# Fused HGRN2 attention and SERF feed-forward: an early weight piece, another rounding rate, masks on VectorE, clamps apart from the logs, and the last store in two parts

## The chip, the cores and the metric

The kernel runs on one core of a Trainium2 chip. The time is device time in microseconds of one launch; a run is one execution, and the median of the runs counts. The profile is of one execution of its own.

## The reference

```python
def _attn_ref(q, k, v, f_logit):            # each (4, 8, 768, 48)
    f = 1.0 / (1.0 + np.exp(-f_logit))
    state = np.zeros((B, H, D, D))
    for t in range(S):
        state = f[:, :, t, :, None] * state + einsum('bhd,bhe->bhde', k[:, :, t], v[:, :, t])
        y[:, :, t] = einsum('bhd,bhde->bhe', q[:, :, t], state)

def _moe_ref(x, w_in, w_out):               # (3072, 384), (384, 2048), (2048, 384)
    h = x @ w_in
    sp = np.maximum(h, 0.0) + np.log1p(np.exp(-np.abs(h)))
    return (h * erf(sp)) @ w_out            # x is y with the heads side by side
```

The inputs q, k, v and f_logit are float32. The two weights are float64; the kernel reads them as pairs of 32-bit words and rounds them to float32 itself.

## The kernel before

The sequence is cut into 24 chunks of 128 tokens, six per batch entry. Two chunks form a block of 256 tokens, so there are 12 blocks. A chunk g passes four stages, each a function:

- `stage_d(g)` multiplies the logs of the decays (`lt`) with a triangle on TensorE (L380), takes two exponentials on ScalarE (`dp` L383, `kd` L386), sends the decays of both half chunks to `Tall` by eight small DMAs (L391, from chunk 3 on), and scales q and k on VectorE (`qd` L395, `kd` L399).
- `stage_t(g)` transposes both on TensorE (L411) and copies them out of PSUM: `qA` on ScalarE (L418), `kT` on ScalarE (L420) up to chunk 8 and on VectorE (L422) after.
- `stage_s(g)` computes the state's increments (L460) and the scores (L468). The scores are masked by a triangle: on VectorE in four instructions (L496), or, for chunks 3 to 9, copied by ScalarE in four instructions (L488) and masked by GpSimd in two (L491). Then the state of the half chunk is updated on VectorE (L438, L439, two of each); the state of the other half is left to the next `stage_t`.
- `stage_y(g)` multiplies scores and state with q (L525) and ScalarE copies the result into `xT` (L529).

Ahead of `stage_d`, `prepare` turns logits into logs of the decays: VectorE clamps them (L360), then ScalarE takes Exp (L364) and Ln (L365). For the first two blocks this is done per chunk.

The feed-forward part of a block is `hidden(blk, gi)` for four groups gi: twelve products of `xT` with `w_in_sb` (L587), each two records in the profile, a copy out of PSUM (L594), and the activation in steps: Exp (L157), two Tanh (L160), two VectorE products (L165), a Tanh (L559) and the last product (L561). The projection with w_out is `project_first` (L670) for blocks 0 and 1 and `project` (L718) after, which needs seven products in place of eight and sums of weights (`sum_w`, L615) and of activations.

A weight is loaded in pieces (`load_piece`, L292, eight of w_in with 768 KB each, then eight of w_out) and rounded by `round_piece`: a copy on ScalarE (L311) and six VectorE instructions (L313, L317, L322, L326, L331, L336). `weights_step` issues one of these seven at a time. Piece p of w_in serves the products of two of the sixteen column tiles, so group 0 of a block needs pieces 0 and 1, group 1 needs 2 and 3, and so on.

Nothing is scheduled at run time: every engine and every DMA queue executes its instructions in the order in which the program issues them, and SP's queue issues almost all DMAs. After an opening written out by hand, with loads, the stages of chunks 0 to 2 and ten rounding steps, a loop over rounds `it` walks a generator of products ("slots": one product of L587, L670 or L718 each). Round 0 has 96 slots in the order of groups h0[0], h0[1], h1[0], h0[2], h1[1], h0[3], h1[2], h1[3] of blocks 0 and 1, round 1 the 48 of block 2, round 2 the 48 of block 3 and then the 32 of the first projection. After given slots (`at`) the loop issues the next stage from `todo`; `prepare` for a later block goes 14 slots ahead of that block's first `stage_d`; and a counter `due` grows by a rate per slot and issues one rounding step whenever it reaches one.

Two products of the stages and of the hidden groups take turns in two PSUM buffers each (`ps_at` for d, t and y; `ps_moe` for hidden groups and projections). The last projection adds its seven partial products (`plus`, L726) and writes 256 rows by one DMA (`store`, L654).

Of the kernel before, what the change touches and what calls it, by code (L numbers as in the profile page):

```python
# [43 lines left out]
FP32 = mybir.dt.float32  # L44
# [26 lines left out]
P = 128  # L71
# [3 lines left out]
def kernel(  # L75
# [10 lines left out]
    nc = tc.nc  # L86
# [142 lines left out]
    def load(g, what="qkv", queue=None):  # L229
        b, c = divmod(g, NCH)  # L230
        queue = queue or nc.sync
        for src, t, n in ((q, qns[g % NQ], "q"), (k, kns[g % NQ], "k")):
            if n in what:
                queue.dma_start(out=t[:].rearrange("t (h d) -> t h d", d=D), in_=heads(src, b, c))
        if "v" in what:
            queue.dma_start(
                out=vts[g % NV][:].rearrange("t (h d) -> t h d", d=D), in_=heads(v, b, c)
            )
# [104 lines left out]
    def use_exp_ln():  # L343
        if sets[0] == EXP_LN:
            return
        sets[0] = EXP_LN
        nc.scalar.add_instruction(
            mybir.InstLoadActFuncSet(
                act_func_set_id=EXP_LN, name=nc.get_next_instruction_name(),
                engine=mybir.EngineType.Activation, ins=[], outs=[],  # L350
            )
        )
# [1 line left out]
    def other_set():  # L354
        sets[0] = 0

    def prepare(blk, j0, j1):

        lt = lts[blk][:, j0:j1, :].rearrange("t j c -> t (j c)")
        nc.vector.tensor_scalar(  # L360
            out=lt, in0=lt, scalar1=LOGIT_MIN, scalar2=None, op0=ALU.max
        )
        use_exp_ln()
        nc.scalar.activation(out=lt, in_=lt, func=AF.Exp, scale=-1.0)  # L364
        nc.scalar.activation(out=lt, in_=lt, func=AF.Ln, bias=1.0)  # L365

    busy = []

# [74 lines left out]
    def stage_s(g):  # L443
        b, n = divmod(g, NCH)
        last = n == NCH - 1
        if n == 0:
            for r in range(2):
                nc.gpsimd.memset(svs[g % NSV][rows(r), r, 0, :, PAD : PAD + D], 0.0)
        qA, kT = qAs[g], kTs.pop(g)
        ps = ps_sc.tile([P, 2, 512], FP32, name="sc", tag="sc")  # L450

        sc = ps[:, :, 0 : HP * C].rearrange("s r (a t) -> s r a t", t=C)
        dS = ps[:, :, HP * C : HP * (C + D)]
        totals = ps[:, 0, HP * (C + D) : HP * (C + D) + 2 * HP]
        vt, kd = vts[g % NV], kds[g % 2]
        for a in range(HP):
            for c in range(1 if last else 2):
                for r in range(2):
                    h = 2 * a + r
                    nc.tensor.matmul(  # L460
                        dS[rows(r), c, D * a : D * (a + 1)],
                        lhsT=kd[half(c), h, 0:D], rhs=vt[half(c), D * h : D * (h + 1)],
                        start=True, stop=True,
                    )
        for a in range(HP):
            for r in range(2):
                for c in range(2):
                    nc.tensor.matmul(  # L468
                        sc[half(c), r, a, :], lhsT=kT[rows(r), a, half(c)],
                        rhs=qA[rows(r), r, a, half(c)], start=True, stop=True,  # L470
                    )
        if g < FIRST:

            pairs = dps[g % 2][:].rearrange("t (a r) d -> t a (r d)", r=2)
            for a in range(HP):
                nc.tensor.matmul(
                    totals[:, 2 * a : 2 * a + 2], lhsT=pairs[:, a, :], rhs=ident[:, C - 1 : P : C],
                    start=True, stop=True,
                )
            nc.vector.tensor_copy(  # L480
                out=Tall[:, g].rearrange("p c a -> p a c"),
                in_=totals.rearrange("p (a c) -> p a c", c=2),
            )
        for c in range(2):
            for r in range(2):
                if FIRST <= g < 2 * ADJACENT:

                    nc.scalar.copy(out=qA[half(1 - r), r, :, half(c)], in_=sc[half(c), r])  # L488
                    if c == 1:
                        flat = qA[half(1 - r), r].rearrange("s a (c t) -> s (a c) t", c=2)  # L490
                        nc.gpsimd.affine_select(  # L491
                            out=flat, in_=flat, pattern=[[0, 2 * HP], [1, C]], compare_op=ALU.is_ge,
                            fill=0.0, base=0, channel_multiplier=-1,
                        )
                    continue
                nc.vector.tensor_tensor(  # L496
                    out=qA[half(1 - r), r, :, half(c)], in0=sc[half(c), r],
                    in1=tri1[half(c)].unsqueeze(1).broadcast_to((C, HP, C)), op=ALU.mult,
                )
        next_state(2 * g, dS)  # L500
        if not last:
            late[g] = lambda: next_state(2 * g + 1, dS)
# [149 lines left out]
    def store(blk):  # L652
# [3 lines left out]
            in_=rows_sb[:, 0:4, :].rearrange("p (t two) c -> p t (two c)", t=CPB),  # L656
        )

    def project_first(blk):

        ops = ps_moe.tile([P, 2, 512], FP32, name="ops", tag="moe")
        for gi in range(n_g):
            gr = groups[blk, gi]
            for tt in range(CPB):
                for j in range(FG):
                    ft = gi * FG + j
                    assert n_pieces + ft * n_pieces // n_ft in rounded
                    while not gr["done"]:
                        act_step()
                    nc.tensor.matmul(  # L670
                        ops[:, tt, 0:d_model],
                        lhsT=gr["h"][:, j, tt * P : (tt + 1) * P],
                        rhs=w_out_sb[:, ft, :],
                        start=(ft == 0), stop=(ft == n_ft - 1),
                    )
                    if j == FG - 1 and tt == CPB - 1:
                        if blk == 0:
                            to_sum.append(sum_w(gi))
                        if gi == n_g - 1:
                            nc.scalar.copy(  # L680
                                out=rows_sb[:, 0:4, :].rearrange("p (t two) c -> p t (two c)", t=CPB),
                                in_=ops[:, :, 0:d_model],
                            )
                            store(blk)
                    yield

    def project(blk):
# [6 lines left out]
            1: (0, 0, 0), 2: (0, 1, 0), 6: (0, 1, 1), 5: (1, 0, 0), 7: (1, 0, 1), 3: (2, 1, 0), 4: (2, 1, 1),  # L694
        }.items()}
        first = [1, 2, 5, 3]

        def pair(n):
            i, j = {2: (0, 1), 5: (1, 0), 3: (2, 1)}[n]
# [37 lines left out]
        def fives():  # L737

            plus(o[:, 3:5, :], o[:, 4:5, :].broadcast_to((P, 2, DH)), pair(5))

        yield from products((2, 3), (5, 7))
        if end:

            fives()
        yield from products((2, 3), (3, 4))
        if not end:
            fives()
        plus(o[:, 1:3, :], o[:, 3:5, :], pair(3))
        plus(o[:, 3, :], o[:, 3, :], place[7])
        store(blk)  # L750
# [42 lines left out]
    with tc.manual_schedule():  # L793
# [5 lines left out]
        load(0, "kv", nc.scalar)  # L799
        load(0, "q")  # L800
        load_f(1)
        load(1, "qk")
        load_f(2)
        load_piece(0)
        load(1, "v")
        load(2)
        load_piece(1)
        load_piece(2)
        load_f(3)
        nc.gpsimd.memset(tri[:], 1.0)  # L810
# [45 lines left out]
        def weights_steps(n):  # L856
            for _ in range(n):
                weights_step()
# [5 lines left out]
        keep_busy(6)  # L864
        prepare(0, 1, 2)
        stage_t(0)
        load(3, "qk")
        load_piece(3)
        stage_d(1)
# [43 lines left out]
        for it in range(n_blocks):  # L913
            gen, n = slots(it)
            if it == 0:
                todo = [(stage_s, 2), (stage_y, 2), (stage_d, 3), (stage_t, 3), (stage_s, 3), (stage_y, 3),
                        (stage_d, 4), (stage_t, 4), (stage_d, 5), (stage_s, 4), (stage_t, 5),
                        (stage_y, 4)] + stages(2)[4:]
                at = [1, 5, 6, 12, 16, 23, 34, 42, 48, 52, 60, 74, 76, 80, 88, 94]
            else:  # L920
                todo = stages(it + 2) if it + 2 < n_blocks else []
                at = [n * x // 48 for x in (2, 6, 11, 17, 25, 29, 34, 41)] if it == 1 else [int(3 + (n - 13) / max(1, len(todo)) * i) for i in range(len(todo))]
# [5 lines left out]
                prepare_at = at[todo.index((stage_d, (it + 3) * CPB))] - 14  # L928
            at, todo = deque(at), deque(todo)
            for s, _ in enumerate(gen):  # L930
                due += (1 if s < 42 else 0.6 if s < 72 else 0.3) if it == 0 else 0.42 if it == 1 else 0.6
                while due >= 1:
                    weights_step()
                    due -= 1
# [2 lines left out]
                if at and s == at[0]:  # L937
# [3 lines left out]
                    if f in (stage_y, stage_y_s):  # L941
# [3 lines left out]
                        if g == 2:  # L945
                            load(5, "v")
                            load_piece(7)
                if it == 0 and s == 14:
                    prepare(2, 0, CPB)
                if it == 0 and s == 9:  # L950
                    load_f(6)
                    load_f(7)
                if s == n // 2 and it + 4 < n_blocks:
                    for j in range(CPB):
                        load_f((it + 4) * CPB + j)
                if it + 3 < n_blocks and s == prepare_at:
                    prepare(it + 3, 0, CPB)
                if it < 2:
                    step = it == 1 and s % 6 == 3
                elif it == 2:  # L960
# [240 lines left out]
```

## Time and profile before

| | us |
|---|---|
| median of 5 runs (lowest, highest) | 619.28 (618.65, 619.62) |
| the profiled execution | 619.4 |
| its span, first to last instruction | 617.6 |
| TensorE busy / VectorE / ScalarE / GpSimd | 586.9 / 460.5 / 382.4 / 14.4 |
| mean granted TensorE clock | 0.985 |
| L587 products, 1152 records | 265.2 |
| six VectorE rounding instructions of a piece, start to start | 4.64 |

A timeline row reads: start, duration, engine, line, operation, output and inputs, shapes, count, and in brackets the idle time before it with what ended it. A window row reads: stretch and length, busy time of the engines with instruction counts, granted clock, share of the DMA engines, GB/s. Durations of overlapping instructions can reach into each other, so repeated instructions are best counted start to start.

### The profile page before, as it was taken

The numbers are of one execution on the slowest core, as the hardware profiler recorded it, in microseconds if no ns is written. First come the engines' busy times: TensorE is split into PE (matmuls) and PEld (weight loads), VectorE is DVE, ScalarE is ACT, GpSimd is POOL, SyncE is SP. The second block draws the span as 40 slices with busy tenths as digits, with TensorE's granted clock in tenths as the row PEclk, the third lists the DMA queues.
The fourth block names the chain that finished last, engine by engine and source line by source line (L and its number), as shares of the span: only waits on it lengthen the run. The fifth ranks groups of instructions, "written<-read, shape, count | busy, mean of one in ns | idle before, by whom it ended". The sixth has DMA issues, their size and how long they took to land.

```text
span 617.6 us, 13765 instructions
## 1 busy us (share of the span) xinstructions
PE 586.9 (95%) x5729; PEld 513.3 (83%) x5729; DVE 460.5 (75%) x784; ACT 382.4 (62%) x483; POOL 14.4 (2%) x33
## 2 busy tenths in 40 slices
PE   8778799999999999999999999999999999999995
PEld 7656688888655689989989989988988989989995
DVE  5998998697489597896796876896886785647551
ACT  5735357987875778775866685875765566366000
POOL 1000001010000000000000000000000000000000
PEclk9978799999999999999999999999999999999999
DMA  9998753351241223223233132142120000000000
GB/s 198 249 234 215 205 157 62 62 102 16 50 78 27 49 56 52 44 61 54 39 65 53 34 71 53 19 86 53 18 62 14 3 27 0 28 1 0 27 27 29
DMA packets 155587, 41.35 MB, mean 67 GB/s; under 512 B 147328, under 2 KB 150400, under 8 KB 155520
## 3 DMA queue, kind: packets, MB, share of 16 engines
q1 hardware_dynamic: 153440, 40.02, 29.7%
q8 instruction: 47, 0.77, 0.5%
q10 hardware_dynamic: 2080, 0.39, 0.3%
q14 instruction: 20, 0.16, 0.1%
HBM read 35.59 MB, written 4.72 MB: 65 GB/s over the span
## 4 chain that ended last, share of the span: by engine, by line
PE 74%; DVE 14%; ACT 7%; issue 3%; DMA 1%; POOL 0%; ACTq 0%; DVEq 0%; SPq 0%; POOLq 0%
PE hps L587 31%; PE ops L718 25%; PE ops L670 7%; PE y L525 3%; PE ps_t L411 3%; PE ps_d L380 2%; ACT x L160 1%; PE sc L468 1%; PE sc L460 1%; DVE sv L438 1%; DVE sv L439 1%; DVE Hg L561 1%; DVE w_in_sb L322 1%; DVE w_in_sb L336 1%; DVE qA L496 1%
## 5 line engine op out<-in xcount | busy, mean ns | idle before, releaser
L587 PE MATMUL hps<-xT,w_in_sb 128*128 128x256 f32 x1152 | 265.2, 386 | 4.2 <-DVE w_in_sb L336 1.9
L587 PEld LDWEIGHTS hps<-xT,w_in_sb 128*128 128x128 f32 x1152 | 219.1, 193 | 38.6 <-ACT xT L529 2.7
L165 DVE SCALAR_TENSOR_TENSOR e<-x,e 128x1024 f32<-128x1024 f32 x96 | 117.0, 1219 | 13.1 <-ACT x L160 12.6
L160 ACT ACTIVATE x<-Hg,serf_bias 128x1024 f32<-128x1024 f32 x88 | 97.5, 1140 | 0.2
L157 ACT ACTIVATE e<-Hg 128x1024 f32<-128x1024 f32 x44 | 46.5, 1058 | 61.7 <-DVE Hg L561 57.6
L718 PE MATMUL ops<-wT,Hg 128*128 128x192 f32 x320 | 78.9, 328 | 0.0
L561 DVE TENSOR_TENSOR Hg<-Hg,e 128x1024 f32<-128x1024 f32 x44 | 53.8, 1222 | 22.2 <-ACT e L559 22.1
L718 PE MATMUL ops<-wT,scratch 128*128 128x192 f32 x288 | 67.8, 326 | 0.9 <-DVE scratch L726 0.9
L718 PE MATMUL ops<-w_out_sb,Hg 128*128 128x192 f32 x320 | 65.1, 326 | 0.0
L594 ACT COPY Hg<-hps 128x1024 f32<-128x1024 f32 x44 | 44.4, 1009 | 32.8 <-PE hps L587 32.4
L718 PEld LDWEIGHTS ops<-wT,Hg 128*128 128x128 f32 x320 | 55.8, 190 | 1.9
L718 PEld LDWEIGHTS ops<-w_out_sb,Hg 128*128 128x128 f32 x320 | 54.6, 190 | 2.0
L559 ACT ACTIVATE e<-e 128x1024 f32<-128x1024 f32 x48 | 50.3, 1049 | 1.9 <-DVE e L165 1.8
L718 PEld LDWEIGHTS ops<-wT,scratch 128*128 128x128 f32 x288 | 50.3, 190 | 1.1 <-issue 1.1
L496 DVE TENSOR_TENSOR qA<-sc,tri 64x256 f32<-64x256 f32 x68 | 28.7, 422 | 24.5 <-PE sc L468 23.6
L726 DVE TENSOR_TENSOR scratch<-scratch,ops 128x384 f32<-128x384 f32 (+1 forms) x40 | 20.1, 503 | 31.8 <-ACT scratch L734 24.5
L525 PEld LDWEIGHTS y<-qA,sv 128*32 128x32 f32 x1536 | 24.2, 111 | 20.7 <-issue 12.9
L525 PE MATMUL y<-qA,sv 128*32 128x64 f32 x1536 | 29.0, 223 | 12.1 <-issue 4.5
L418 ACT COPY qA<-ps_t 64x512 f32<-64x512 f32 x48 | 27.7, 577 | 19.6 <-PE ps_t L411 19.2
L395 DVE TENSOR_TENSOR qd<-qn,dp 128x384 f32<-128x384 f32 x24 | 13.3, 556 | 32.7 <-ACT dp L383 28.6
L718 PE MATMUL ops<-w_out_sb,scratch 128*128 128x192 f32 x144 | 35.2, 326 | 0.0
L438 DVE TENSOR_TENSOR sv<-sc,sv 48x192 f32<-48x192 f32 x80 | 28.4, 355 | 8.7 <-ACT qA L488 7.3
(111 smaller groups left out, 645.6 us busy)
## 6 DMA issues: line engine op xcount, KB each, us to landing
lt<-in_f_logit_dram SPq DMA_DIRECT2D x24, 192.0 KB, 3.7
qn<-in_q_dram SPq DMA_DIRECT2D x24, 192.0 KB, 3.3
out_dram<-scratch SPq DMA_DIRECT2D x12, 384.0 KB, 2.6
kn<-in_k_dram SPq DMA_DIRECT2D x23, 192.0 KB, 3.5
vt<-in_v_dram SPq DMA_DIRECT2D x23, 192.0 KB, 3.6
sv<-in_v_dram SPq DMA_DIRECT2D x84, 48.0 KB, 2.9
w_out_sb<-in_moe_w_in_dram SPq DMA_DIRECT2D x4, 768.0 KB, 6.3
Hg<-in_moe_w_in_dram SPq DMA_DIRECT2D x4, 768.0 KB, 6.9
```

The lines of the kernel that those rows point to most:

```text
L157: nc.scalar.activation(out=dst[:], in_=h, func=AF.Exp)
L160: nc.scalar.activation(out=dst[:], in_=h, func=AF.Tanh, bias=serf_bias[:, i : i + 1], scale=SERF_KAB[i][0])
L165: nc.vector.scalar_tensor_tensor(out=e[:], in0=x[:], scalar=SERF_KAB[i][2], in1=e[:], op0=ALU.add, op1=ALU.mult)
L438: nc.vector.tensor_tensor(out=new, in0=add, in1=old, op=ALU.add)
L496: nc.vector.tensor_tensor(out=qA[half(1 - r), r, :, half(c)], in0=sc[half(c), r], in1=tri1[half(c)].unsqueeze(1).broadcast_to((C, HP, C)), ...
L525: nc.tensor.matmul(y[M * i : M * (i + 1), kt, half(c)], lhsT=sv[:, r, c, a, o : o + M], rhs=qA[:, r, a, half(c)], start=(n == 0), stop=Tru ...
L559: nc.scalar.activation(out=e[:], in_=e[:], func=AF.Tanh, scale=SERF_C)
L561: nc.vector.tensor_tensor(out=h, in0=h, in1=e[:], op=ALU.mult)
L587: nc.tensor.matmul(hps[:, j, :], lhsT=w_in_sb[:, kt, ft * P : (ft + 1) * P], rhs=xTs[blk][:, kt, :], start=(kt == 0), stop=(kt == n_k - 1),)
L594: nc.scalar.copy(out=gr["h"], in_=hps[:])
L670: nc.tensor.matmul(ops[:, tt, 0:d_model], lhsT=gr["h"][:, j, tt * P : (tt + 1) * P], rhs=w_out_sb[:, ft, :], start=(ft == 0), stop=(ft == ...
L718: nc.tensor.matmul(place[n], lhsT=x[:, j, :], rhs=y, start=(gi == 0 and j == 0 and n in first), stop=(gi == n_g - 1 and j == 1), skip_grou ...
```

## The change

- `prepare` is split into `clamp` (VectorE) and `logs` (ScalarE). In the loop the clamp goes six slots ahead of the logs. For block 2 they go after slots 18 and 24, where both went after 14.
- Masks: only chunks 3 to 5 still go over ScalarE and GpSimd; chunks 6 to 9 use the four VectorE instructions.
- Opening loads: the first w_in piece goes ahead of chunk 1's q, k and v, and the second ahead of chunk 2's logits, q, k and v.
- Two rounding steps are added after `stage_t(0)`; the rate of round 0 is 1 up to slot 18, 0.46 up to 66 and 0.3 after, where it was 1 up to 42, 0.6 up to 72 and 0.3 after; the rate of round 1 is 0.55 (was 0.42) and of later ones 0.55 (was 0.6).
- Round 0 takes `stage_d(3)` ahead of `stage_y(2)`, and moves four of its sixteen stages by one to three slots.
- The last projection keeps product 4 in a PSUM tile of its own, finishes the sum of the first 128 rows before the last four products, and stores 128 rows from SP and 128 from ScalarE.

```diff
-    def prepare(blk, j0, j1):
-
+    def clamp(blk, j0, j1):
         lt = lts[blk][:, j0:j1, :].rearrange("t j c -> t (j c)")
         nc.vector.tensor_scalar(
             out=lt, in0=lt, scalar1=LOGIT_MIN, scalar2=None, op0=ALU.max
         )
+
+    def logs(blk, j0, j1):
+
+        lt = lts[blk][:, j0:j1, :].rearrange("t j c -> t (j c)")
         use_exp_ln()
         nc.scalar.activation(out=lt, in_=lt, func=AF.Exp, scale=-1.0)
         nc.scalar.activation(out=lt, in_=lt, func=AF.Ln, bias=1.0)
+
+    def prepare(*which):
+        clamp(*which)
+        logs(*which)
...
-                if FIRST <= g < 2 * ADJACENT:
+                if FIRST <= g < 2 * FIRST:
...
+    def store_tile(blk, t, queue):
+        r = blk * TB + t * P
+        queue.dma_start(
+            out=out[r : r + P, :],
+            in_=rows_sb[:, 2 * t : 2 * t + 2, :].rearrange("p two c -> p (two c)"),
+        )
...
+        if end:
+            place[4] = ps_at.tile([P, 512], FP32, name="ops4", tag="at")[:, 0:DH]
+            first.append(4)
...
         if end:
 
             fives()
+            yield from products((2, 3), (3,))
+            plus(o[:, 1, :], o[:, 3, :], place[3])
+            store_tile(blk, 0, nc.sync)
+            plus(o[:, 3, :], o[:, 3, :], place[7])
+            yield from products((2, 3), (4,))
+            plus(o[:, 2, :], o[:, 4, :], place[4])
+            store_tile(blk, 1, nc.scalar)
+            return
         yield from products((2, 3), (3, 4))
-        if not end:
-            fives()
+        fives()
...
         load_f(1)
-        load(1, "qk")
+        load_piece(0)
+        load(1, "qkv")
+        load_piece(1)
         load_f(2)
-        load_piece(0)
-        load(1, "v")
         load(2)
-        load_piece(1)
         load_piece(2)
...
         stage_t(0)
+        weights_steps(2)
         load(3, "qk")
...
-                todo = [(stage_s, 2), (stage_y, 2), (stage_d, 3), (stage_t, 3), (stage_s, 3), (stage_y, 3),
+                todo = [(stage_s, 2), (stage_d, 3), (stage_y, 2), (stage_t, 3), (stage_s, 3), (stage_y, 3),
...
-                at = [1, 5, 6, 12, 16, 23, 34, 42, 48, 52, 60, 74, 76, 80, 88, 94]
+                at = [1, 5, 8, 12, 16, 23, 36, 43, 48, 52, 60, 74, 76, 80, 88, 94]
...
-                due += (1 if s < 42 else 0.6 if s < 72 else 0.3) if it == 0 else 0.42 if it == 1 else 0.6
+                due += (1 if s < 18 else 0.46 if s < 66 else 0.3) if it == 0 else 0.55
...
-                if it == 0 and s == 14:
-                    prepare(2, 0, CPB)
+                if it == 0 and s == 18:
+                    clamp(2, 0, CPB)
+                if it == 0 and s == 24:
+                    logs(2, 0, CPB)
...
+                if it + 3 < n_blocks and s == prepare_at - 6:
+                    clamp(it + 3, 0, CPB)
                 if it + 3 < n_blocks and s == prepare_at:
-                    prepare(it + 3, 0, CPB)
+                    logs(it + 3, 0, CPB)
```

## The prediction

> **What bounds the kernel now.** I read the page's busy rows first, then its slices, then the chain of waits.
>
> ```profile
> PE 586.9 (95%) x5729; PEld 513.3 (83%) x5729; DVE 460.5 (75%) x784; ACT 382.4 (62%) x483; POOL 14.4 (2%) x33
> ...
> PE   8778799999999999999999999999999999999995
> ...
> DVE  5998998697489597896796876896886785647551
> ...
> PEclk9978799999999999999999999999999999999999
> ```
>
> TensorE is full from the sixth slice (15.4 us each) on, and the chain of waits from 192 to 347 us is nearly all TensorE. Only the first 77 us, a little between 111 and 191, and the end can give anything. In the first slices VectorE is the full row. Windows of VectorE say how full:
>
> ```profile
> 13.00:65.37 52.37, 47.50 (x90) 0.90 0.91 230
> 65.37:102.00 36.63, 34.30 (x54) 0.91 0.58 152
> 65.37:152.68 87.31, 73.19 (x116) 0.96 0.43 96
> 102.00:152.68 50.68, 38.89 (x63) 1.00 0.33 56
> 152.68:190.00 37.32, 26.85 (x38) 1.00 0.30 55
> ```
>
> (length, VectorE busy, instructions, clock, DMA share, GB/s). So VectorE rests only 4.9 us of the first stretch, 11.8 us of 102 to 152.68 and 10.5 us of the last. The worst stall stands in the timeline:
>
> ```profile
> 63.26 0.81 PE L380 MATMUL ps_d<-lt,tri 128*128 128x384 f32 x2
> ...
> 64.49 0.49 ACT L386 ACTIVATE kd<-ps_d 128x384 f32<-128x384 f32 x1
> ...
> 70.92 0.55 DVE L395 TENSOR_TENSOR qd<-qn,dp 128x384 f32<-128x384 f32 x1
> ...
> 71.61 1.09 PE L411 MATMUL ps_t<-ident,qd 128*128 128x128 f32 x4 [4.09 <-DVE qd L395]
> ...
> 73.35 4.60 PE L587 MATMUL hps<-xT,w_in_sb 128*128 128x256 f32 x12
> ```
>
> Chunk 4's decays are ready at 64.6, but its product qd starts at 70.92, behind 5.6 us of rounding. TensorE waits 4.1 us, and then twelve records take 4.4 us where the warm rate needs 2.6 (28 took 6.05 at 85.83).
>
> Below, d, t, s, y are a chunk's four stages; a slot is one L587 product, two records, 0.433 us; P0 to P15 are weight pieces in the order of rounding; a piece costs VectorE 4.64 us (L313 at 64.22 to the next at 68.86). Lines are those of before. I followed the changed program's order on each engine with these durations, start to start.
>
> **Loads, first piece.** The trace's landings: f1 7.58, q1 8.48, k1 9.29, f2 10.38, P0 13.29, v1 14.04, v2 16.74, P1 20.37. They come one after another, so differences are prices: P0 2.9, q1, k1, v1 2.4 together, P1 2.9 to 3.6, a chunk's f 0.65 to 1.1. The new order f1, P0, q1, k1, v1, P1, f2 puts f2 at 7.58 + 2.9 + 2.4 + 3.2 + 0.7 = 16.8 (16.4 to 18.4). Its clamp ran at 12.89 and VectorE takes it in order, with chunk 0's masks and states behind it. So VectorE starts this stretch 3.9 us later, with P0's first two steps (1.15 us) already done in its idle time. On ScalarE the logs wait likewise, with chunk 0's four v copies and t(1)'s copies behind. q1 and k1 land 3 us later (11.4, 12.2), and P0's copy L311 (0.9) now stands ahead of d(1)'s exponentials, which end near 13.3: both come before 16.8, and f2's wait hides them; were f2 early they would cost 0.9 to 1.6.
>
> What follows costs 47.5 us less 1.15: 16.8 + 0.35 + 46.35 = 63.5 at the earliest, 65.3 by pitches, to the second step of P6. Before reached the same row at 65.37 after the same 90 rows, because it spent 4.9 us waiting. On the way y(1) ends at 30.1, the first slot starts at 30.65 (before 27.64, **+3.0**), state 3 ends at 56.55 (55.57), slot 24 starts at 57.8 (56.88, **+0.9**).
>
> **Rounding rate.** One step per slot now falls to 0.46 from slot 18, not 0.6 from slot 42. Thus qd(4) follows P6's second step directly. TensorE: 13 slots from 57.8 are 5.6, plus 1.6 for the cool clock that the same place had before (22 records took 6.4 where 4.8 is warm), so d(4) starts at 65.0; the exponentials end at 66.7, qd and kd at 67.25; seven more slots, and t(4) runs 68.7 to 69.6 instead of 71.61 to 73.5. TensorE never cools there. To the end of t(5) are 17 slots (7.4), d(5), s(4), t(5) (0.65, 1.0, 0.87): 79.6 against 85.83, **-6.2**. P7 is ready at 80.8, wanted at 81.8: one microsecond of cover; if it is gone, that much is lost.
>
> The Trainium skill's page "TensorE: Matmul & The Clock Gate" (section What's actually happening) says the clock halves only after an idle window of about 3.4 us; the trace shows 0.53 at 36 to 38 us after gaps of 2.3 and 1.0 us. By the rule the 3 us gap ahead of y(3) would stay warm and the forecast would be 615.0.
>
> **The debt.** Steps put off come back. By 102 us before has begun the thirteenth piece, the changed order the eleventh: 9.3 us more to come. The masks of chunks 6 to 8 add 3 x 1.76 (four L496, start to start) = 5.3; 4.5 (an L165 1.1, an L561 1.2, a pair of states 1.5, a kT copy 0.7) now fall behind L360's clamp for chunks 10 and 11. So 38.9 + 9.3 + 5.3 - 4.5 = 49.0 us, 50 by pitches, without rest, from qd(7), which must await d(7) (101.4) and the exponential (102.6). It ends near 152.6; before reached that clamp at 152.68. The early gain is thus eaten: y(7) stands behind its masks and state and ends at -5.5, y(8) at -3.2; slot 36 of the third round waits for ScalarE's copy L594, behind the logs, behind the clamp: 155.3 against 156.85, -1.5.
>
> After that the 10.5 us of rest cover chunk 9's masks (1.76) and the 4.5 carried over; without that cover the first projection's last group would come 6.3 us later. ScalarE loses 1.51 us of L488 copies per chunk, so the copy L418 that frees y(9)'s PSUM comes at 173.4, not 176.28; but the last group of the first projection waits for L561, which ended at 184.0 and now at 182.3. From there TensorE is continuous: **-1.8** stays. GpSimd's masks (1.4 to 2.0 us) vanish off the path.
>
> **Edits with one answer.** Clamps six slots earlier: free where VectorE rests, nothing gained while it is in debt; if moved wrongly, 0.55 us each. d(3) ahead of y(2) puts its eight decay DMAs (0.65 each on SP) ahead of v loads and the eighth w_in piece; that lands some 6 us later and is first touched near 71: hidden. The new PSUM tile takes a buffer idle since 494: nothing.
>
> **Last store.**
>
> ```profile
> 610.76 0.49 PE L718 MATMUL ops<-wT,Hg 128*128 128x192 f32 x2
> 611.29 0.94 DVE L726 TENSOR_TENSOR scratch<-scratch,ops 128x384 f32<-128x384 f32 x2 [2.05 <-PE ops L718]
> 612.26 0.37 SPq L654 DMA_DIRECT2D out_dram<-scratch  x1
> ```
>
> Only one 0.35 us addition remains after the last product, so the second store issues at 611.65: -0.6. Whole stores landed 2.4 to 4.2 us after issue, this one 3.8. The second is issued by ScalarE, whose two issues at the start took 0.48 and 0.69 us where SP takes 0.37. A half should take 2.2 to 3.8; I take 3.5, nearest to this store's own row: **-0.9** in all (-0.4 to -2.2).
>
> [...]
>
> **Sum.** The profiled execution took 619.4 (span 617.6 and 1.8 around it), 0.1 above the median 619.28. 619.4 - 1.8 - 0.9 - 0.1 = 616.6.
>
> **Rivals.** *The debt hides* (20%): VectorE's 11.8 us of rest in 102 to 152.68 absorb it, and -6.2 stands: 612.2. Against: 49 to 50 us of work wait behind qd(7), and 50 us is all the stretch has. *The debt waits* (13%): VectorE in that stretch is held by ScalarE's copies and tanh inputs as before. If half of the 11.8 us of rest stays, TensorE is 5.9 later than forecast: 622.5; it decides once more than about 4 us of rest stay. For it: L165's 12.6 us of waits for L160. *The edits cancel* (17%): slower start and debt eat all but the store: 618.4. The likeliest case has 50%, with 614.5 to 618.4 of its own.
>
> A measurement here tells 0.2% (1.2 us) from no change. Faster: 0.48 of the first, 0.20, and 0.04 of the cancelling case, 0.72; within 0.2%: 0.15; slower 0.13. The range runs from half a microsecond beyond the hiding case to a little beyond no change, 611.6 to 620.2; most of the waiting case and some of the hiding one are left out.
>
> **What would show it.** Right: first slot near 30.7; f2's clamp near 17; qd(4) near 66; t(5) ended near 79.6; VectorE without rest from 103 to 152; y(7) and y(8) waiting for it; the second store issued 0.4 us after the last product. Wrong: f2 landing after 19.5 wipes out the gain; L360 for chunks 10 and 11 far from 152; TensorE cold again after slot 43.

## The result, and the profile after

The changed kernel takes 622.01 us (median of 21 runs, 619.78 to 624.5) against 619.25 of before: ratio 1.0042, 95% interval 1.0033 to 1.005, so slower by 2.8 us where 2.7 less were forecast, and above the range of 611.6 to 620.2. The profiled execution took 623.1 (span 621.4). In the changed kernel the lines have moved: clamp L359 (was L360), logs L367 and L368 (L364, L365), and from there to the hidden part seven lines down: qd L402 (L395), transposes L418 (L411), qA copies L425 (L418), kT copy L429 (L422), state L445 and L446 (L438, L439), score copies L495 (L488), y L532 (L525), hidden products L594 (L587), copies L601 (L594), Tanh L566 (L559), last activation product L568 (L561). The first projection is L684 (L670), the store in two parts L668. Kernels made from the one before keep its lines.

The slices of the page, and VectorE in the windows that were shown for before:

```profile
PE   7777999993999999999999999999999999999995
...
DVE  4999777999499588796896785896886795657551
...
PEclk9998999998899999999999999999999999999998
```

```profile
65.37:102.00 36.63, 25.89 (x43) 1.00 0.62 158
102.00:152.68 50.68, 48.42 (x79) 0.97 0.31 53
```

TensorE's hole in the fifth slice is gone, and a deeper one (a 3) stands in the tenth, at 140 to 155 us. VectorE now rests 10.7 us in 65 to 102, where before it rested 2.3, and 2.3 us in 102 to 152.68, where it rested 11.8: work was moved out of the one into the other. Both halves show in TensorE's times against the profile of before: the first slot starts 1.8 us later, slot 24 0.4 later, t(5) ends 6.4 earlier, y(7) starts 7.0 earlier (124.64 for 131.68), y(8) 3.4 later (155.01 for 151.65), and from the second half of the first projection on everything is 3.72 later, to the last product.

The early half, in the timeline (start, duration, engine, line, operation):

```profile
57.28 7.57 PE L594 MATMUL hps<-xT,w_in_sb 128*128 128x256 f32 x26 [0.57 <-ACT xT L536]
...
66.05 0.56 DVE L402 TENSOR_TENSOR qd<-qn,dp 128x384 f32<-128x384 f32 x1 [1.42 <-ACT dp L390]
...
68.35 0.60 PE L418 MATMUL ps_t<-ident,qd 128*128 128x128 f32 x4
```

qd(4) waits for its exponential and no more for rounding, and t(4) follows without a hole. The late half, in the same view (in brackets the idle time before the row, and what ended it):

```profile
155.01 2.03 PE L532 MATMUL y<-qA,sv 128*32 128x64 f32 x64 [9.23 <-ACT qA L425]
```

In the kernel before, the same stretch ran in this order:

```profile
148.06 1.22 DVE L561 TENSOR_TENSOR wT<-wT,e 128x1024 f32<-128x1024 f32 x1
...
149.31 1.06 ACT L157 ACTIVATE e<-wT 128x1024 f32<-128x1024 f32 x1 [1.98 <-DVE wT L561]
150.38 1.17 ACT L418 COPY qA<-ps_t 64x512 f32<-64x512 f32 x2
...
151.65 1.21 PE L525 MATMUL y<-qA,sv 128*32 128x64 f32 x64 [0.86 <-issue]
...
152.68 0.56 DVE L360 TENSOR_SCALAR lt<-lt 128x768 f32<-128x768 f32 x1
```

For the changed kernel the chain of waits that ended last says why, piece by piece:

```profile
151.12 0.55 DVE lt L359
151.67 1.14 DVE wT L568
...
153.80 0.56 ACT qA L425
...
156.15 1.28 ACT L347
...
157.44 0.85 ACT lt L367
...
159.18 1.01 ACT Hg L601
```

y(8) has its scores and its state by 148.2. But it writes into a PSUM buffer that t(9) held, and that only ScalarE's copies L425 of t(9) give back. ScalarE takes its orders in turn, and ahead of L425 stands the exponential L157 of the next hidden group, which needs the buffer `e` that VectorE's L568 gives back. L568 stands in VectorE's queue behind seven rounding steps, chunk 8's masks and the clamp: ScalarE rested 7.55 us before L157. Before, the same chain was there, but its wait was 0.86 us: y(8) started 0.1 us after L418 had ended. Behind L425 in turn stand a Tanh, a table load, the logs and L601, the copy that frees the PSUM for slot 36 of this round. The sixteen records of L594 after y(8), from 156.97 on, took 5.37 us where sixteen from 132.00 on took 3.62; the granted clock was 0.51 in 150 to 157.

The last store:

```profile
615.40 0.37 ACTq L668 DMA_DIRECT2D out_dram<-scratch  x1
```

The second half is issued 0.6 us earlier against the last product than the whole store was, but in this execution it landed 4.1 us after its issue, where the whole store had taken 3.8.

### The profile page after: what moved, and what is told of

It is laid out like the page before. It is cut to its first block, busy times and chain, and to the rows that moved or that the text cites. A ratio compares the mean times of both kernels' runs of the same rounds, so it can differ in the third digit from the quotient of the medians.

```text
span 621.4 us, 13742 instructions
## 1 busy us (share of the span) xinstructions
PE 585.3 (94%) x5729; PEld 511.8 (82%) x5729; DVE 466.5 (75%) x801; ACT 376.5 (61%) x467; POOL 8.4 (1%) x25
## 4 chain that ended last, share of the span: by engine, by line
PE 71%; DVE 14%; ACT 5%; DMA 3%; issue 3%; SPq 3%; DVEq 0%; ACTq 0%
PE hps L594 32%; PE ops L735 25%; PE ops L684 4%; PE y L532 3%; PE ps_t L418 2%; PE ps_d L387 2%; DMA lt<-in_f_logit_dram 1%; ACT x L160 1%; DVE qA L503 1%; PE sc L467 1%; DVE sv L445 1%; PE sc L475 1%; DMA Tall<-dp 1%; DVE sv L446 1%; DVE Hg L568 1%
## 5 line engine op out<-in xcount | busy, mean ns | idle before, releaser
L594 PE MATMUL hps<-xT,w_in_sb 128*128 128x256 f32 x1152 | 263.9, 385 | 5.4 <-DVE w_in_sb L336 2.7
L594 PEld LDWEIGHTS hps<-xT,w_in_sb 128*128 128x128 f32 x1152 | 217.8, 192 | 39.4 <-DVE w_in_sb L336 3.9
L157 ACT ACTIVATE e<-Hg 128x1024 f32<-128x1024 f32 x44 | 46.5, 1058 | 68.7 <-DVE Hg L568 59.7
L568 DVE TENSOR_TENSOR Hg<-Hg,e 128x1024 f32<-128x1024 f32 x44 | 53.8, 1222 | 22.5 <-ACT e L566 22.4
L601 ACT COPY Hg<-hps 128x1024 f32<-128x1024 f32 x44 | 44.4, 1008 | 37.5 <-PE hps L594 37.1
L503 DVE TENSOR_TENSOR qA<-sc,tri 64x256 f32<-64x256 f32 x84 | 35.5, 422 | 27.6 <-PE sc L475 26.2
L566 ACT ACTIVATE e<-e 128x1024 f32<-128x1024 f32 x48 | 50.3, 1048 | 1.9 <-DVE e L165 1.8
L532 PEld LDWEIGHTS y<-qA,sv 128*32 128x32 f32 x1536 | 24.5, 112 | 25.5 <-ACT qA L425 10.9
L532 PE MATMUL y<-qA,sv 128*32 128x64 f32 x1536 | 29.8, 225 | 16.6 <-ACT qA L425 10.0
L402 DVE TENSOR_TENSOR qd<-qn,dp 128x384 f32<-128x384 f32 x24 | 13.4, 557 | 34.1 <-ACT dp L390 34.0
L425 ACT COPY qA<-ps_t 64x512 f32<-64x512 f32 x48 | 27.7, 577 | 18.4 <-PE ps_t L418 18.0
L445 DVE TENSOR_TENSOR sv<-sc,sv 48x192 f32<-48x192 f32 x80 | 28.4, 355 | 4.9 <-ACT qA L495 3.5
```

The lines of the kernel that those rows point to most:

```text
L157: nc.scalar.activation(out=dst[:], in_=h, func=AF.Exp)
L425: nc.scalar.copy(out=qAs[g][half(r), r], in_=pss[0][half(r)])
L445: nc.vector.tensor_tensor(out=new, in0=add, in1=old, op=ALU.add)
L503: nc.vector.tensor_tensor(out=qA[half(1 - r), r, :, half(c)], in0=sc[half(c), r], in1=tri1[half(c)].unsqueeze(1).broadcast_to((C, HP, C)), ...
L532: nc.tensor.matmul(y[M * i : M * (i + 1), kt, half(c)], lhsT=sv[:, r, c, a, o : o + M], rhs=qA[:, r, a, half(c)], start=(n == 0), stop=Tru ...
L566: nc.scalar.activation(out=e[:], in_=e[:], func=AF.Tanh, scale=SERF_C)
```

## The experiments

The theory: the early gain is real; the loss is the put-off rounding, done in VectorE's order ahead of an L568 that ScalarE, and through it two PSUM buffers, wait for. The rivals: the masks, the opening loads, or the split store make the loss by themselves. Ratios are to the kernel before on the same chip, with 95% intervals.

**One part alone, on the kernel before.** Four kernels take one part each; in the first only the last store is split, as in the diff above.

> The kernel before with the last store in two parts and nothing else. The forecast's term: 0.9 us off, 618.4. What the changed kernel's trace suggests instead: the second half is issued 0.6 us earlier against the last product but lands 4.1 us after its issue where the whole store took 3.8, and the span closes 1.9 us after the landing where it closed 1.5 after: no gain, 619.0 to 619.5. If the split costs time by itself: 620 or more.

617.89 us, ratio 0.9972 (0.9959 to 0.9984): a gain of 1.4, more than forecast, and my reading of the changed kernel's trace missed. In this run's profile the second half was issued at 611.35 and landed 2.3 us later, not 4.1.

```diff
-                if FIRST <= g < 2 * ADJACENT:
+                if FIRST <= g < 2 * FIRST:
```

> The kernel before with the masks of chunks 6 to 9 on VectorE and nothing else. Theory (the 11.8 us that VectorE rested in 102 to 152 us hold three masks of 1.76, and y no longer waits for GpSimd, 2.1 us in two waits): 618 to 619.3. Rival (the masks by themselves push L561 back and make the loss at y(8)): 620.5 to 622.

618.16 us, ratio 0.9984 (0.9971 to 0.9996): the masks gain a little, inside the theory's range. VectorE was busy for 45.63 of the 50.68 us in which it had been busy for 38.89, and TensorE lost nothing there.

The third takes the rates of the changed kernel with the moved stages of round 0:

```diff
-                due += (1 if s < 42 else 0.6 if s < 72 else 0.3) if it == 0 else 0.42 if it == 1 else 0.6
+                due += (1 if s < 20 else 0.46 if s < 66 else 0.3) if it == 0 else 0.55
```

> The kernel before with the rounding rates of the changed kernel (1 up to slot 20 in place of the two steps added earlier), d(3) ahead of y(2) and the four moved stages; loads, masks, clamps and store as before. Theory: the early gain appears (t(5) ends 6 to 7 us earlier than 85.8) and is given back between 140 and 155, where L561 and ScalarE's L157 wait behind rounding: y(8) later than 151.65; end 620.5 to 623. Rival (the rates gain by themselves and only the masks, the clamps or the loads spoil it): 613 to 616.

619.7 us, ratio 1.0007 (0.9993 to 1.002): no difference, below what the theory gave. The two halves are there and cancel: t(5) ends 8.6 us earlier than before, and at y(8) all but 1.1 of it is gone. y(8) starts 0.1 us after the copy L418 of t(9) has ended, which stood behind an L157 that had waited 3.8 us for L561.

```profile
150.51 1.80 PE L525 MATMUL y<-qA,sv 128*32 128x64 f32 x56 [7.16 <-issue]
```

The fourth takes the new load order and the two rounding steps behind t(0):

```diff
-        load(1, "qk")
-        load_f(2)
         load_piece(0)
-        load(1, "v")
+        load(1, "qkv")
+        load_piece(1)
+        load_f(2)
         load(2)
-        load_piece(1)
         load_piece(2)
...
         stage_t(0)
+        weights_steps(2)
```

> The kernel before with the changed order of the opening loads and the two early rounding steps, nothing else. Theory: first slot 1.5 to 2 us later, VectorE ahead by two steps, qd(4) still behind the rounding; at most 1 us of the start reaches the end: 619.3 to 620.5. Rival (the loads cause the loss): 621.5 to 622.5. Rival (the loads are what lets t(4) come early): under 617.

623.89 us, ratio 1.0075 (1.0057 to 1.0093): 4.6 us slower, more than any theory gave. The first slot is 1.7 us late, which was expected. What was not: VectorE, which takes the clamp of chunk 2 at 15.53 instead of 12.89 and has two more steps in its queue, comes to the clamp of chunks 4 and 5 at 51.90 instead of 49.70, ScalarE's logs wait for it, and chunk 3's score copies behind the logs come at 55.00 instead of 52.01. GpSimd masks what they copied, and y(3) waits for that: 4.3 us in all, where it was 2.1 before. The rest of the loss was not followed. The logs' row, and then from the list of waits from 30 to 80 us (total, times, longest):

```profile
52.48 0.85 ACT L364 ACTIVATE lt<-lt 128x768 f32<-128x768 f32 x1 [3.95 <-DVE lt L360]
```

```profile
PE y L525 <- POOL qA L491: 4.3, 2, 3.9
```

The four parts come to -0.28, -0.16, +0.07 and +0.75%, together +0.38; the whole change has +0.42. That the two agree is chance, as the next runs show: put together, the parts cost other amounts than alone. The clamps apart from the logs have no run of their own. In the late chain the clamp of chunks 10 and 11 puts L568 off by 0.5 us (151.12 to 151.59).

**One part undone, on the changed kernel.** First the masks:

> The changed kernel with the masks of chunks 6 to 9 back on ScalarE and GpSimd. Theory (VectorE's backlog holds L568 at 151.6, so ScalarE's L157, so the copies of t(9), so the PSUM of y(8)): three masks fewer ahead of that L568 are 5.3 us, less the 1.5 us that VectorE waits per chunk for the copies; y(8) at 150 to 152 instead of 155.0, the end 3 to 4.5 us earlier, 617.5 to 619. Rival (the rounding alone makes the loss, the masks fit in VectorE's rests): within 1 us of 622.0.

621.69 us, ratio 1.003 (1.0017 to 1.0044), against 1.0042 with the masks on VectorE: the time is the rival's, and my sum for the masks falls. L568 came at 151.56, as with them. Two waits of VectorE between 80 and 152 us:

```profile
DVE w_out_sb L313 <- ACT w_out_sb L311: 3.6, 1, 3.6
...
DVE sv L443 <- ACT qA L495: 0.8, 1, 0.8
```

In the changed kernel the first was 0.3 and the second absent. So 4.1 of the 5.3 us freed on VectorE became waits for ScalarE, which got four copies per chunk more. The unbroken run of VectorE only starts later, at 119.0 instead of 102.4.

Then the loads (the diff of e7 reversed, and a rate of 1 up to slot 20):

> The changed kernel with the opening loads of before; the two early rounding steps go behind slot 18 (rate 1 up to 20). Theory (with the new rates the load order costs what the rates-only kernel had more at t(5), about 2 us, and VectorE's unbroken run from qd(7) to L568 starts that much earlier): 619.5 to 620.5. Rival (the loads cost here what they cost by themselves, 4.6): 617 to 618. Rival (they cost nothing, the wall at y(8) is set by later work alone): 621.5 to 622.5.

618.83 us, ratio 1.0007 (0.9995 to 1.002). As a time this lies between the theory and the first rival; by the ratios the loads cost 0.35% here, some 2.2 us, near the theory's size. TensorE had them all back by d(5) and more (67.85 for 71.38, 3.5 us), lost 1.7 to a piece of w_in that was not rounded in time at 79.8, and stood at y(8) as long as ever (9.23 us), 2.1 earlier. Without the loads the rest of the change is worth nothing (+0.07%), where its parts alone come to -0.37%: the hole at y(8) eats the early gain and what the store gains.

**The place and the amount of the debt.** Two kernels leave the work as it is and move it:

```diff
-                due += (1 if s < 18 else 0.46 if s < 66 else 0.3) if it == 0 else 0.55
+                due += (1 if s < 18 else 0.46 if s < 60 else 0.6) if it == 0 else 0.5 if it == 1 else 0.55
```

> The changed kernel with the rounding rate 0.6 instead of 0.46 and 0.3 from slot 60 of the first round on, 0.5 in the second: some 9 steps (7 us) are done between 66 and 102 us, where VectorE rested 10.7 us. Theory (the debt is paid where it stalls TensorE, and could be paid where VectorE rests): t(5) still ends near 79.5, L568 of 151.6 comes 6 to 7 us earlier, y(8) at 148 to 150, end 616 to 617.5. Rival (those rests are waits for ScalarE and the steps only delay qd(6) and qd(7) there): L402 of d(7) later than 102.4, TensorE stalls near 100, end 621 to 623.

616.38 us, ratio 0.9941 (0.9927 to 0.9955): inside the theory's range. t(5) ended 1.0 us later than in the changed kernel, L568 started 5.5 us earlier, and the hole fell from 9.2 to 4.0:

```profile
146.13 1.22 DVE L568 TENSOR_TENSOR wT<-wT,e 128x1024 f32<-128x1024 f32 x1
...
149.56 2.03 PE L532 MATMUL y<-qA,sv 128*32 128x64 f32 x64 [3.96 <-ACT qA L425]
```

The other puts the seven steps that stood ahead of L568 behind t(9)'s kT copy:

```diff
-                due += (1 if s < 18 else 0.46 if s < 66 else 0.3) if it == 0 else 0.55
+                due += (1 if s < 18 else 0.46 if s < 66 else 0.3) if it == 0 else 0.55 if it == 1 or s < 4 else 0 if s < 20 else 1
```

> The changed kernel with the last seven rounding steps (5.7 us of VectorE) held back from slot 4 of the third round to slot 20, which puts them behind the copy L429 of t(9) instead of ahead of the L568 that ran at 151.6. Nothing is taken away, only the place changes. Theory: L568 at about 146, L425 of t(9) at 148, y(8) at 148.5 instead of 155.0, TensorE's wait of 9.2 us falls to 2 to 3; the steps then fill the 6.2 us of rest at 157 to 163; end 616 to 618. Rival (VectorE's total up to the first projection decides, not the place): the last L568 of group (0,3) stays at 186.5, end within 1 us of 622.0.

617.75 us, ratio 0.9954 (0.9936 to 0.9972). Nothing was taken away, only the place changed, and 0.9% came back. y(8) was at 150.1, not 148.5, since L568 (146.72) still stands behind masks, state and clamp, and TensorE's wait was 3.96 us, not 2 to 3. The last activation came 1.9 us late for the first projection, and its next records ran slowly (16 took 7.12 where the changed kernel took 5.43):

```profile
182.91 7.12 PE L684 MATMUL ops<-w_out_sb,wT 128*128 128x384 f32 x16 [1.89 <-DVE wT L568]
```

**ScalarE's order.** If the chain is right, y(8) can be set free without touching VectorE at all. In this kernel VectorE's order is the changed kernel's; on ScalarE, L425 of t(9) and one L157 change places:

```diff
+                if it == 2:
+                    at[2] = 17
```

> The changed kernel with t(9) issued after slot 17 of the third round instead of 19. VectorE's order stays; on ScalarE only the copies L425 of t(9) and the L157 that waited 7.6 us change places. Theory (y(8) waits for a PSUM buffer that L425 frees, and L425 stood behind L157, behind L568): y(8) at 147 to 149 instead of 155.0; but the L601 that frees the third round's slot 36 still stands behind L157 and the logs, at 157 to 159: half or less of it reaches the end, 620 to 621.5. Rival (y(8) waits for VectorE's state or masks): y(8) at 153 or later, the time unchanged. Rival (y(8) alone decides): 615 to 616.5.

619.08 us, ratio 1.0005 (0.9991 to 1.0019); the gain on the changed kernel is 0.37%, a little more than expected. y(8) came 8.2 us earlier, and the hole moved to slot 36, whose PSUM waits for L601:

```profile
146.82 0.75 PE L532 MATMUL y<-qA,sv 128*32 128x64 f32 x32 [0.63 <-ACT qA L425]
...
159.45 1.22 PE L594 MATMUL hps<-xT,w_in_sb 128*128 128x256 f32 x2 [6.93 <-ACT Hg L601]
```

This is the run that decides: masks, state and L568 stood within 0.4 us of where they had been, and y(8) no longer waited for L568 or the masks. For the state it waited 0.31 and 0.48 us. Next the logs of chunks 10 and 11 go where ScalarE waited anyway (e12 on the changed rates, e10 with the rates of e3; both with t(9) after slot 17):

```diff
                     prepare_at = at[todo.index((stage_d, (it + 3) * CPB))] - 14
+                if it == 2:
+                    prepare_at = 6
```

> The changed kernel with only the second half of e10: t(9) after slot 17, and for chunks 10 and 11 the clamp after slot 0 and the logs after slot 6; the rounding rates, and so the debt, as changed. Theory (VectorE's debt keeps L568 near 151, but y(8) and slot 36 no longer stand behind it in full): y(8) near 147, the copy L601 for slot 36 at 154 to 156 instead of 159.2, the end 3 to 4.5 us below e8's 619.1: 614.5 to 616. Rival (the debt alone sets the end of the activations, so the last L568 of group (0,3) keeps its place): 618.5 to 619.5. Rival (with ScalarE in order the debt costs nothing): 610 to 611 as e10.

614.71 us, ratio 0.993 (0.9916 to 0.9944), inside the expected 614.5 to 616. The wait at slot 36 fell from 6.93 to 3.37 us.

> The rates that pay the debt early (0.6 from slot 60, 0.5, 0.55), and in the third round the clamp for chunks 10 and 11 after slot 0, their logs after slot 6 (in 7 us in which ScalarE waited) and t(9) after slot 17. Theory (what is left at y(8) and slot 36 is ScalarE's order: L425 behind L157, L601 behind the logs and a second table load, 4.3 us): y(8) at 146 to 147, slot 36 not waiting, end 612.5 to 615. Rival (the last L568 of group (0,3) is the bound by then and stays): within 0.7 of 616.4.

610.13 us, ratio 0.9857 (0.9841 to 0.9874), better than the theory's 612.5 to 615. The two holes are nearly closed: y(8) waits 0.63 us, slot 36 (the last product of the sixteen records behind it) not at all, and a smaller wait of 1.85 us stands ahead of y(8).

```profile
142.28 2.42 PE L594 MATMUL hps<-xT,w_in_sb 128*128 128x256 f32 x10 [1.85 <-ACT Hg L601]
145.33 1.20 PE L532 MATMUL y<-qA,sv 128*32 128x64 f32 x64 [0.63 <-ACT qA L425]
146.46 3.72 PE L594 MATMUL hps<-xT,w_in_sb 128*128 128x256 f32 x16
```

Last, the same with the opening loads of before:

> The kernel of e10 with the opening loads of before. Theory: with the debt paid early, the 2 us that the load order costs at t(5) reach the end: 1 to 2.5 us below e10, 611 to 613.5. Rival (what VectorE and ScalarE still have to do ahead of the first projection decides): the same as e10 within 0.7.

607.96 us, ratio 0.9831 (0.981 to 0.9853), the lowest of the study. Its five runs lie at 607.1 to 612.9: in the slowest, which is the profiled one, four waits of L594 for rounded pieces of w_in come to 9.2 us (2.7 in e10). So its opening may be on the edge, which one profile does not show. The median is 2.2 us below e10's, the distance that the theory gave, but the intervals overlap: between theory and rival this kernel does not decide, and the two are not told apart.

## Why the prediction was wrong

**Right.** The bound and the early path held nearly to the row. Forecast and profile after: f2's clamp 16.8 and 15.62 (its landing was 1.2 us earlier than the price list gave); first slot 30.65 and 29.44; slot 24 57.8 and 57.28; qd(4) near 66 and 66.05; t(4) 68.7 and 68.35; end of t(5) 79.6 and 79.4; y(7) ending 5.5 earlier than before and 5.8. So was the debt: 49 us of unbroken work from qd(7), and the clamp at 152.6; VectorE worked 47.34 of the 49.3 us from 102.3 on and reached the clamp at 151.12.

**The step that failed** is the next one in the same part: "4.5 (...) now fall behind L360's clamp". I entered those instructions as relief, and let y(8) wait for its masks and state alone and slot 36 for the logs behind the clamp alone. One of the four is the L568 that frees ScalarE's L157. Before, it ran at 148.06, ahead of its clamp; now it ran at 151.59, behind it, and L425, the logs and L601 with it. I had followed each queue's order, but not which wait on ScalarE ends last once VectorE's queue is full. Forecast: y(8) ending 3.2 us earlier than before, slot 36 at 155.3. Measured: y(8) starting 3.4 us later and ending 4.2 later, and the copy L601 for slot 36 ending at 160.2. The trace of before had the wait that I left out: y(8) stood 0.86 us and started when L418 had ended. e8 shows the link through L425, e12 and e10 the one through logs and L601.

**The later cover.** I held that 10.5 us of rest behind 152 cover what is left; the last L568 of group (0,3) was to end at 182.3. It ended at 187.7, and the projection stood on it 1.3 us. The rest was there (VectorE worked 27.82 of those 37.32 us), but in the wrong place: 6.2 us of it are one wait for ScalarE's L566, which is itself behind the logs. Before had the same wait, with 5.9 us.

**The rivals.** *The debt waits* had 622.5, close to the time, for the wrong reason: VectorE was to rest, and it rested 2 us. *The debt hides* was refused on the right ground. No rival had VectorE full and ScalarE waiting in order behind it.

**The loads** were priced against before, at +0.9 by slot 24, and are no term of their own in the sum: the forecast's -6.2 holds them. Their own price is 2.2 us in the changed kernel (e9) and 4.6 alone (e7); without them the early gain is larger (8.6 in e6). **The masks** were 5.3 us of VectorE's work as entered, but not 5.3 us of delay: with them or without, L568 came at 151.6 (e2), because ScalarE's copies in their place made VectorE wait. **The store** had the right sign and was too small: 0.9 forecast, 1.4 measured alone. In that profile the half landed in 2.3 us where I took 3.5; in the changed kernel's it took 4.1, and there the split gained nothing (6.4 us from the last product to the end of the span, 6.35 before).

**The skill's rules.** The Trainium skill's page "DMA: Bandwidth & Descriptors" (section Rules for kernel authors) advises against two transfers to disjoint halves of the partitions, since both use the same 16 engines. Each half of this store covers all 128 partitions and the first starts earlier, so the rule does not settle it; e1 gains 1.4 us. The page "TensorE: Matmul & The Clock Gate" (section What's actually happening) has the clock fall after about 3.4 us of idleness. Waits of 1.85 us (e10) and 2.26 (e12) left it up. Waits of 3.96 (e3) and 9.23 brought it down, as the page says, and so did one of 3.37 in e12: two records still ran at full rate, then sixteen took 5.26 us where 3.62 is warm, with 0.50 granted in 156 to 158. But it also fell in e4 after a wait of 1.89 us (the sixteen records shown above, 0.66 granted in 183 to 186). And at 57.28 the 26 records took 7.4 us, start to start, where 5.6 is warm, after gaps of only 1.8, 0.5 and 0.6 us. The cold 1.6 us that I had booked there by the row of before, against that section's rule, were right.

## What to carry to other kernels

Work that is put off must be placed, not only counted: find the last instruction of another engine that stands behind it in the queue, and follow that engine's own queue to the buffers that it gives back. With seven rounding steps ahead of one product TensorE stood for 9 us; doing some nine of them in VectorE's earlier rests, or those seven behind the copy that follows, brought back 1.0 and 0.9%. And put what can run early (here the clamp and the logs) into an engine's known waits, ahead of the instruction that it would wait for: with the debt paid early and t(9) two slots sooner this made the change worth 1.4% against before.

## What the runs showed of the hardware

The last store lands in two ways. In the profiles of kernels with two halves, the second landed 2.2 to 2.3 us after its issue in five of them (e1, e2, e3, e8, e11) and 3.5 to 4.1 us in four (the changed kernel, e4, e9, e10). From that issue to the end of the span it is 4.4 to 4.8 us in the five and 5.4 to 6.0 in the four; e12, whose landing the profile does not show, has 6.2. Whole stores took 3.8, 4.5 and 4.7 to land (before, e5, e7). Each of these kernels was profiled once, so whether one kernel lands in both ways from run to run is not shown, and what decides it stays open.
